# Weight conversion in an attention and two-FFN kernel: other ticks, engines and queues for its steps

## The chip, the cores and the metric
The kernel runs on one core of a Trainium2 chip. The metric is the device time of one execution in microseconds (us). PE is the matrix engine, DVE, ACT and POOL are the vector, scalar and GpSimd engines, and SP is the engine that issues nearly all DMAs; DMA engines move the data on their own.

## The reference
Three stages follow each other. Attention over 4 batches of 8 heads: 32 global and 512 local positions with 64 numbers each; a global query sees everything, a local query sees the global keys and a window of 32 positions to each side. Then a feed-forward net with the square of a ReLU, and another whose activation is a rational function:

```python
    out_g = np.matmul(sm(s_g), v_all)
    mask = np.abs(pos[:, None] - pos[None, :]) <= window
    s_ll = np.where(mask, s_ll, -1000000000.0)
    a_l = sm(np.concatenate([s_lg, s_ll], axis=-1))
    out_l = np.matmul(a_l, np.concatenate([v_g, v_l], axis=2))
...
    x = np.ascontiguousarray(attn_out.transpose(0, 2, 1, 3)).reshape(B * S, H * D)
    r = np.maximum(x @ w_in, 0.0); x = (r * r) @ w_out
    P = a[0] + a[1] * h + a[2] * h2 + a[3] * h3
    Q = 1.0 + np.abs(b[0]) * np.abs(h) + np.abs(b[1]) * h2
    g = P / (Q + 1e-06); return g @ w_out
```

There are 2176 tokens, the model width is 512 and the inner width 2048. The weights arrive as 64-bit floats.

## The kernel before, in words
**Stages.** Attention runs in 40 groups i (0 to 39), five for each of eight half batches n of four heads: four groups of 128 local positions and one for the global queries. For each group do_S makes scores, ACT exponentials (L705, L729, L730), do_T transposes, do_PV multiplies by v, and do_xT transposes the result into xT, the tokens of the FFNs. prep transposes q and k of a later half batch; ACT copies the results (L661, L664, L666). From i = F0 = 11 on a "fill job" of FFN1 is mixed into each group (f_h, f_low, f_y), for the first 5 of 16 chunks f of the inner width; each fifth one, at i = 16, 21, 26 and so on, copies its sums to two tiles pk (L502, one by DVE, one by ACT) and stores them to a DRAM buffer, park (L503). FFN1 (76 jobs) and FFN2 (96 jobs) are then run by step(k), one job a step: do_h multiplies a chunk of w_in with 384 tokens, relu2 or rat_a, rat_b, rat_c compute the activation on ACT and DVE, do_y multiplies with w_out.

**Weights.** PE works with a weight as two parts, hi and lo. A chunk f has two halves, and each half is an item that goes through a pipeline. A "wide" item is loaded with its 64-bit words (L131, tile S), and ACT takes the upper words' absolute value (L138, tile T), POOL scales the lower words (L146), DVE clamps, shifts and puts the sign back (L141, L152, L156), POOL adds (L161), ACT makes hi (L170) and the engine cv["lo"] makes lo (L176): POOL during attention, DVE afterwards. Items that are needed only later are "spilled": the f32 result is stored to DRAM (L166) and loaded again as an "f32" item (L127), for which only hi and lo are left to do. NSET says up to which chunk of FFN1 this is done in attention.

**What sets the order.** cv_tick advances the pipeline. Every cv["per"] ticks a new item is loaded (w_load), and each item runs a step when its age in ticks is the number in its table: OX at first, OE from group 15 on, OL for wide items in the FFNs, OS for f32 items. A group of attention has 4 ticks up to i = 14, then 2 or 3; a step of the FFNs has as many as step says in `ticks`. All T tiles, and the two pk tiles too, come from one pool, cv3, of four slots, so a step that needs a slot waits for the last user of it. Each engine runs its instructions in the order in which they are written. DMAs share eight completion semaphores; one that reuses a semaphore waits for the landing of the DMA that used it last.

**First loads.** The string "kGqAgKQB" orders them: k of half batch 0, k of the global positions, q, v in nine parts (L550, L551, L553), q of the global positions, k and q of half batch 1, then four copies of v within SBUF (L559 to L562), all issued by SP.

Of the kernel before, what the change touches and what calls it, by code (L numbers as in the profile page):

```python
# [9 lines left out]
F32 = mybir.dt.float32  # L10
# [3 lines left out]
ALU = mybir.AluOpType  # L14
# [9 lines left out]
def kernel(  # L24
# [17 lines left out]
    B, H, SL, D = q_l.shape  # L42
    SG = q_g.shape[2]
    T = SL + SG
# [3 lines left out]
    NF = DFF // 128  # L48
# [3 lines left out]


    NPRE, NPART, NSUB = 5, 1536, 256
    NSET = 11
    REST = (384, 256)
    GRP = (384, [384] * 5 + [256])
    NMAX = 384
# [1 line left out]
    pe, ve, sc, gp, sy = nc.tensor, nc.vector, nc.scalar, nc.gpsimd, nc.sync  # L60
# [111 lines left out]
    def w_lo(it):  # L172
        ph, f, half = it["k"]
        if not it["spill"]:
            w = wt[ph, f]
            cv["lo"].tensor_tensor(out=w[:, 1, half], in0=it["T"], in1=w[:, 0, half].bitcast(F32), op=ALU.subtract)  # L176
            done.add(it["k"])

    pools["a"] = wpre
    done = set()  # L180
    todo, line, cv = [], [], dict(z=0, n=0, at=None, per=4, lo=gp)

    def items(ph, fs, mode, spill=False):
        return [dict(k=(ph, f, half), mode=mode, spill=spill) for f in fs for half in range(2)]
# [4 lines left out]
    if wide:  # L189
        back, new = items(0, range(NPRE, NSET), "f32"), items(0, range(NSET, NF), "wide")  # L190
        mixed = back[:6] + new[:1] + back[6:8] + new[1:2] + back[8:] + new[2:]
    else:
        mixed = items(0, rest, "f32")
    plan = [items(0, some, "wide" if wide else "f32"), items(0, range(NPRE, NSET), "wide", True) if wide else [],
            mixed, items(1, rest, "wide", True) if wide else [],
# [3 lines left out]
    LEFT = [sum(len(x) for x in plan[i + 1:]) for i in range(6)]  # L199
# [2 lines left out]

    OX = dict(abs=8, elow=8, clamp=9, shift=9, sign=9, add=10, hi=16, lo=18)
    OE = dict(abs=4, elow=4, clamp=5, shift=6, sign=6, add=8, hi=11, lo=13)
    OL = dict(abs=2, low=3, clamp=3, shift=4, sign=4, add=5, hi=7, lo=9)
    OS = dict(hi=5, lo=8)
# [19 lines left out]
    def cv_idle():  # L228
        return not (todo or line)
# [156 lines left out]
    N1 = sum(j[0] == 0 for j in jobs)  # L386
# [3 lines left out]
    def step(k):  # L390
        last, late = False, []

        if k < NR + 3:
            ticks, stage = (6 - (k > 5) if len(todo) > LEFT[2] else 2), (2 if k < NF else 3)
        elif k < N1 - (NF - NPRE) + 3:
            ticks, stage = 2, 4
        else:
            ticks, stage = (0 if cv_idle() else 6), 5
        left = LEFT[stage]
        if k < NJ:  # L400
            ph, gi, t0, n, f, _, last, _ = jobs[k]
            while (ph, f, 1) not in done:
                cv_tick(left)
            do_h(k)
        if k == N1:
            wide_s.close()
            pools["t"] = ctx.enter_context(tc.tile_pool(name="tmp", bufs=2, side="right"))
        if k + 1 < NJ and last:
            for z in range(1, NK):
                x_split(*jobs[k + 1][:4], z)  # L410
        elif k + 4 < NJ and jobs[k + 4][5]:
            x_split(*jobs[k + 4][:4], 0)


        lag = [2 if y < N1 else 3 for y in ys[:2]]
        if ys and ys[0] <= k - lag[0]:
            do_y(ys.pop(0))
            lag.pop(0)
        while ys and (ys[0] <= k - lag[0] or (last and lag[0] == 2 and ys[0] < k)):
            do_y(ys.pop(0))  # L420
            lag.pop(0)
            lag.append(2 if ys and ys[0] < N1 else 3)
        if k < NJ:
            if ph == 0:
                late = list(relu2(k, k < NF))
                ys.append(k)
            else:
                rat_a(k)
        if N1 <= k - 1 < NJ:
            rat_b(k - 1)  # L430
        if N1 <= k - 2 < NJ:
            rat_c(k - 2)
            ys.append(k - 2)
        while outs:
            outs.pop(0)()

        for t in range(ticks):
            if late and t == 1:
                late.pop(0)()
            cv_tick(left)  # L440
        for f in late:
            f()
# [63 lines left out]
    with ExitStack() as at:  # L506
# [11 lines left out]
        raw1 = wpre.tile([128, 2, 2, 512], F32R, tag="w3", name="raw1").bitcast(F32)  # L518
        raw1 = raw1[:, 0].rearrange("p a (c h d) -> p (a c) h d", h=4, d=D)

        def load_qk(n, i):

            b, hq = divmod(n, 2)
            src, dst, nm = ((q_l, qraw, "qr"), (k_l, kraw, "kr"))[i]
            t = raw1 if n == 1 and not i else raw.tile([128, 4, 4, D], F32, tag=nm, name=nm, bufs=1 + i)
            x = src[b, 4 * hq:4 * hq + 4].rearrange("h (p c) d -> c p h d", c=4)
            for c in range(4):
                sy.dma_start(t[:, c], x[c])
            dst[n] = t


# [8 lines left out]
        def load_v(n, part):  # L540
            b, hq = divmod(n, 2)
            hs = slice(4 * hq, 4 * hq + 4)
            w = vw[n % 2]
            wf = w.rearrange("p w h d -> p w (h d)")
            A, Bw, C = wf[:, 0:5], wf[:, 5:10], wf[:, 10:14]
            vg = v_g[b, hs].rearrange("h g d -> g h d")
            vl = v_l[b, hs]
            if part == 0:
                for a in range(5):
                    sy.dma_start(w[0:96, a, :, 0:D], vl[:, 96 * a:96 * a + 96].rearrange("h p d -> p h d"))  # L550
                sy.dma_start(w[96:128, 9, :, 0:D], vl[:, 480:512].rearrange("h p d -> p h d"))  # L551
                for p, a in ((96, 0), (64, 5), (32, 10)):
                    sy.dma_start(w[p:p + 32, a, :, 0:D], vg)  # L553
                return
            if part == 2:
                for p, t, m in ((96, A, 4), (64, Bw, 4), (32, C, 3)):
                    gp.tensor_copy(t[p:p + 32, 1:], t[p:p + 32, 0:1].to_broadcast([32, m, 4 * (D + 1)]))
                return
            sy.dma_start(Bw[0:64], A[32:96])  # L559
            sy.dma_start(Bw[96:128, 0:4], A[0:32, 1:5])  # L560
            sy.dma_start(C[0:32], A[64:96, 0:4])
            sy.dma_start(C[64:128], A[0:64, 1:5])  # L562
# [13 lines left out]
        for i, pair in enumerate(some):  # L576
            for h in range(4):
# [15 lines left out]
        gr = [wpre.tile([128, 2, 2, 512], F32R, tag="w4", name="gr0").bitcast(F32).rearrange("p a b c -> p (a b c)"),  # L593
              fill(0)]
        gr = [t[0:SG, 0:H * B * D] for t in gr]

        def load_g(i):
            sy.dma_start(gr[i].rearrange("g (x d) -> g x d", d=D), (q_g, k_g)[i].rearrange("b h g d -> g (b h) d"))

        for c in "kGqAgKQB":  # L600
            if c in "qk":
                load_qk(0, "qk".index(c))
            elif c in "QK":
                load_qk(1, "QK".index(c))
            elif c in "gG":
                load_g("gG".index(c))
            else:
                load_v(0, "ABR".index(c))

        ve.memset(xT[:, 0, 0:512], 0.0)  # L610
        wu = bank("PV")
# [58 lines left out]
        F0 = 11  # L670
# [151 lines left out]
        pend = {}  # L822
        cv["at"] = OX

# [11 lines left out]
        for i in range(NS + 1):  # L836
# [55 lines left out]
                sc.activation(coef[:, 6:8], coef[:, 4:6], AF.Abs)  # L892
            if i == F0 + NPRE - 1:
                cv["at"] = OE
            for _ in range(4 if i < F0 + NPRE - 1 else 2 + i % 2):
                cv_tick(LEFT[1])
        do_xT(NS - 1)
        f_y(len(fjobs) - 1)
# [6 lines left out]
    fs.close()  # L905
    cv.update(at=OL, per=3)
    pools["b"] = ctx.enter_context(tc.tile_pool(name="wrest", bufs=1))
    cv["lo"] = ve
    turns.update(y=[2, 5, 3, 6, 4, 7])
    for k in range(NJ + 3):  # L910
        step(k)
# [31 lines left out]
```

## Time and profile before
| | us |
|---|---|
| median of 3 runs | 944.23 (943.25 to 944.95) |
| profiled execution | 944.41 |
| its span | 942.6 |
| PE busy | 900.1 (95%) |
| DVE busy | 722.5 (77%) |
| ACT busy | 611.9 (65%) |
| POOL busy | 156.9 (17%) |

The span is cut into windows, and in each the busy time of the engines is compared with the length of the window; where PE stands still, the timeline says in brackets for how long and which instruction released it. Attention ends at about 242 us, FFN1 at about 540 us.

### The profile page before, as it was taken

Reading aid. Unit: us, or ns where it says so; the run is one execution under the profiler, and the core shown is the slowest. Engines: PE = TensorE matmul, PEld = TensorE weight load, DVE = VectorE, ACT = ScalarE, POOL = GpSimd, SP = SyncE. Lnnn points to the kernel's source line nnn. Section 1 sums busy time; section 2 is a strip of 40 time slices with the busy share of each in tenths; the row PEclk is TensorE's granted clock in tenths of the full one; section 3 lists DMA queues with packets and bytes.
Section 4 is the critical chain, followed back from the end, with each engine's and each line's share of the span. In section 5 each row is a group of like instructions: output and inputs, shape, how many; then the busy total and the mean of one; then the engine's idle time right before and its main releaser. Section 6 shows DMA issues by size and latency. Waiting matters only on the chain.

```text
span 942.6 us, 19526 instructions
## 1 busy us (share of the span) xinstructions
PE 900.1 (95%) x7440; PEld 817.6 (87%) x7440; DVE 722.5 (77%) x1668; ACT 611.9 (65%) x1312; POOL 156.9 (17%) x183
## 2 busy tenths in 40 slices
PE   7869899999999999999999979999999999999997
PEld 4647797989998999999999969888889889888875
DVE  3697876765479576566765598998999999999996
ACT  3567566654677564545554587877777877777875
POOL 5286533310023132221220000000000000000000
PEclk9888999999999999999999999999999999999999
DMA  9999879520555256252421410010010010010010
GB/s 191 194 205 192 201 175 245 149 66 24 158 135 154 88 163 204 90 199 70 148 87 56 133 46 1 1 34 1 1 34 1 1 34 1 1 34 1 3 32 23
DMA packets 101741, 84.21 MB, mean 89 GB/s; under 512 B 60176, under 2 KB 87312, under 8 KB 101648
## 3 DMA queue, kind: packets, MB, share of 16 engines
q1 hardware_dynamic: 101648, 82.97, 33.6%
q8 instruction: 58, 0.95, 0.5%
q14 instruction: 35, 0.29, 0.1%
HBM read 59.51 MB, written 16.52 MB: 81 GB/s over the span
## 4 chain that ended last, share of the span: by engine, by line
PE 70%; DVE 13%; DMA 6%; ACT 5%; issue 2%; SPq 2%; POOL 1%; DVEq 0%; ACTq 0%; POOLq 0%
PE S L286 28%; PE y L364 14%; PE y L361 12%; PE H L471 4%; PE Y L496 4%; DMA S<-in_moe_w_in_dram 2%; PE S L691 2%; DVE big L343 2%; PE PV L785 1%; DVE ts L335 1%; PE tr L658 1%; DVE tq L334 1%; DMA big<-big 1%; DVE T L141 1%; DVE T L156 1%
## 5 line engine op out<-in xcount | busy, mean ns | idle before, releaser
L286 PE MATMUL S<-big,w 128*128 128x384 f32 (+1 forms) x2064 | 364.8, 326 | 1.6 <-ACT big L268 1.1
L286 PEld LDWEIGHTS S<-big,w 128*128 128x128 f32 x2064 | 343.6, 188 | 10.8 <-ACT big L268 1.3
L364 PE MATMUL y<-w,big 128*128 128x512 f32 x816 | 211.0, 398 | 10.2 <-DVE big L343 6.4
L364 PEld LDWEIGHTS y<-w,big 128*128 128x128 f32 x816 | 149.0, 188 | 46.4 <-DVE big L343 16.9
L361 PE MATMUL y<-big,w 128*128 128x384 f32 (+1 forms) x912 | 159.4, 324 | 1.7 <-DVE big L310 1.2
L361 PEld LDWEIGHTS y<-big,w 128*128 128x128 f32 x912 | 149.0, 188 | 2.6 <-DVE big L310 1.9
L161 POOL TENSOR_TENSOR T<-T,S 128x512 uint32<-128x512 uint32 x64 | 88.6, 1384 | 310.0 <-DVE T L156 125.2
L320 ACT ACTIVATE big<-S 128x384 f32<-128x384 f32 (+1 forms) x96 | 45.4, 473 | 83.8 <-PE S L286 73.8
L307 DVE TENSOR_TENSOR big<-big 128x384 f32<-128x384 f32 (+1 forms) x60 | 38.8, 646 | 76.8 <-ACT big L303 76.7
L299 ACT ACTIVATE big<-S 128x384 f32<-128x384 f32 (+1 forms) x76 | 35.4, 466 | 85.1 <-PE S L286 84.5
L323 DVE TENSOR_TENSOR ts<-ts,S 128x384 f32<-128x384 f32 (+1 forms) x96 | 50.8, 529 | 23.5 <-ACT ts L321 23.4
L322 ACT ACTIVATE tq<-big,coef 128x384 f32<-128x384 f32 (+1 forms) x96 | 65.9, 686 | 0.0
L321 ACT ACTIVATE ts<-S,coef 128x384 f32<-128x384 f32 (+1 forms) x96 | 62.3, 648 | 0.0
L324 DVE SCALAR_TENSOR_TENSOR ts<-ts,coef,S 128x384 f32<-128x384 f32 (+1 forms) x96 | 56.8, 592 | 3.4
L303 ACT ACTIVATE big<-big 128x384 fp32r<-128x384 f32 (+1 forms) x76 | 38.2, 503 | 30.3 <-PE y L361 29.7
L138 ACT ACTIVATE T<-S 128x512 f32<-128x512 f32 x64 | 42.8, 670 | 21.8 <-DMA S<-in_moe_w_in_dram 8.9
L336 DVE SCALAR_TENSOR_TENSOR ts<-tq,ts 128x384 f32<-128x384 f32 (+1 forms) x96 | 51.4, 535 | 3.3
L496 PE MATMUL Y<-f,w 128*128 128x256 f32 x360 | 51.4, 293 | 0.0
L310 DVE TENSOR_TENSOR big<-big,big 128x384 fp32r<-128x384 f32 (+1 forms) x76 | 45.8, 603 | 7.2 <-ACT big L305 5.2
L343 DVE TENSOR_TENSOR big<-ts,big 128x384 fp32r<-128x384 f32 (+1 forms) x96 | 50.7, 528 | 0.2 <-ACT big L342 0.2
L325 DVE TENSOR_TENSOR tq<-tq,big 128x384 f32<-128x384 f32 (+1 forms) x96 | 50.7, 528 | 0.0
L471 PE MATMUL H<-f,w 128*128 128x256 f32 x360 | 50.6, 290 | 0.0
(127 smaller groups left out, 1244.9 us busy)
## 6 DMA issues: line engine op xcount, KB each, us to landing
S<-in_moe_w_out_dram SPq DMA_DIRECT2D x32, 512.0 KB, 4.5
scr<-T SPq DMA_DIRECT2D x34, 256.0 KB, 2.2
T<-scr SPq DMA_DIRECT2D x34, 256.0 KB, 2.8
S<-in_moe_w_in_dram SPq DMA_DIRECT2D x32, 256.0 KB, 4.7
S<-in_moe_w_in_dram SPq DMA_DIRECT2D x16, 512.0 KB, 4.0
out_dram<-xT SPq DMA_DIRECT2D x17, 256.0 KB, 2.6
kr<-in_k_l_dram SPq DMA_DIRECT2D x32, 128.0 KB, 5.1
qr<-in_q_l_dram SPq DMA_DIRECT2D x28, 128.0 KB, 4.4
```

The lines of the kernel that those rows point to most:

```text
L161: gp.tensor_tensor(out=u, in0=u, in1=it["S"][:, :, 0], op=ALU.add)
L286: pe.matmul(h, wk[k][s], x[k][t], start=m == 0, stop=m == 3 * NK - 1)
L321: sc.activation(s, h, AF.Identity, scale=coef[:, 3:4], bias=coef[:, 2:3])
L322: sc.activation(q, av, AF.Identity, scale=coef[:, 7:8], bias=coef[:, 6:7])
L323: ve.tensor_tensor(out=s, in0=s, in1=h, op=ALU.mult)
L324: ve.scalar_tensor_tensor(out=s, in0=s, scalar=coef[:, 1:2], in1=h, op0=ALU.add, op1=ALU.mult)
L336: ve.scalar_tensor_tensor(out=s, in0=q, scalar=2.0, in1=s, op0=ALU.subtract, op1=ALU.mult, reverse0=True)
L343: ve.tensor_tensor(out=lo, in0=s, in1=hi.bitcast(F32), op=ALU.subtract)
L361: pe.matmul(y[m][:, 0:n], a, x, start=st and z == 0, stop=sp and z == 2)
L364: pe.matmul(y[m], a, x, start=st and z == 0, stop=sp and z == 2)
L471: pe.matmul(h, w[:, s, 0, 128 * k:128 * k + 128], fx[a, k][t], start=m == 0, stop=m == 3 * NK - 1)
L496: pe.matmul(fy[m // 2][:, NSUB * (m % 2):NSUB * (m % 2) + NSUB], w[:, z % 2, 1, 128 * m:128 * m + 128], (hi, hi, lo)[z], start=f == 0 and ...
```

## The change
Five edits are made at once:
- The first loads are issued from two queues: k, q and v of half batch 0 and the copies stay on SP; k of the global positions, k and q of half batch 1 and q of the global positions are issued by ACT, ahead of everything else that ACT does.
- The counter z starts at 3, so a load is made in the first tick of each group of attention in place of the last, and the table OX counts three ticks more for every step, the first 11 ticks from the load.
- lo (L176) is made by DVE throughout.
- NSET is 12: the two halves of chunk 11 are converted in attention, with one more tick in the even groups after 25, and FFN1 begins with eight wide items and fourteen f32 items in place of ten and twelve. Its steps up to the eighth have 6 ticks.
- At the border to FFN2 three steps have no ticks, and the later ones 3 in place of 6.

```diff
-    NSET = 11
+    NSET = 12
...
-            cv["lo"].tensor_tensor(out=w[:, 1, half], in0=it["T"], in1=w[:, 0, half].bitcast(F32), op=ALU.subtract)
+            ve.tensor_tensor(out=w[:, 1, half], in0=it["T"], in1=w[:, 0, half].bitcast(F32), op=ALU.subtract)
...
-    todo, line, cv = [], [], dict(z=0, n=0, at=None, per=4, lo=gp)
+    todo, line, cv = [], [], dict(z=3, n=0, at=None, per=4)
...
-    OX = dict(abs=8, elow=8, clamp=9, shift=9, sign=9, add=10, hi=16, lo=18)
+    OX = dict(abs=11, elow=11, clamp=12, shift=12, sign=12, add=13, hi=19, lo=21)
...
-            ticks, stage = (6 - (k > 5) if len(todo) > LEFT[2] else 2), (2 if k < NF else 3)
+            ticks, stage = (6 - (k > 8) if len(todo) > LEFT[2] else 2), (2 if k < NF else 3)
...
-            ticks, stage = (0 if cv_idle() else 6), 5
+            ticks, stage = (0 if cv_idle() or N1 <= k < N1 + 3 else 6 if k < N1 else 3), 5
...
-        def load_qk(n, i):
+        def load_qk(n, i, q=sy):
...
-                sy.dma_start(t[:, c], x[c])
+                q.dma_start(t[:, c], x[c])
...
-        for c in "kGqAgKQB":
...
+        load_qk(0, 1)
+        load_g(1, sc)
+        load_qk(0, 0)
+        load_qk(1, 1, sc)
+        load_v(0, 0)
+        load_g(0, sc)
+        load_qk(1, 0, sc)
+        load_v(0, 1)
...
-            for _ in range(4 if i < F0 + NPRE - 1 else 2 + i % 2):
+            for _ in range(4 if i < F0 + NPRE - 1 else 2 + (i % 2 or i > 25)):
```

Four places show how this moves instructions. The first is ACT from its first instruction to its first copy for kt; f and gr are the tiles of the global positions, raw is q of half batch 1.

```order
-L938 UNCONDITIONAL_BRANCH
+L937 UNCONDITIONAL_BRANCH
+L598 DMA f_246<-in_k_g_dram 32x32x64
+L528 DMA kr<-in_k_l_dram 128x4x64 x4
+L598 DMA gr_245<-in_q_g_dram 32x32x64
+L528 DMA raw_109<-in_q_l_dram 128x4x64 x4
 L614 ACT_TABLE_LOAD
 L664 COPY kt_318<-tr 128x5x96
```

Ten DMA issues now stand ahead of the table load and the first copy.

The second is ACT at the park of group 16, before: the park copy, one abs, the exponentials.

```order
L502 COPY pk<-Y 128x512
L138 ACTIVATE T<-S 128x512
L705 ACTIVATE s<-s,nmx 128x128 x4
L664 COPY kt_2066<-tr 128x5x96
L666 COPY kt_2066<-tr 128x32
```

And the same place now.

```order
L502 COPY pk<-Y 128x512
L138 ACTIVATE T<-S 128x512 x2
L705 ACTIVATE s<-s,nmx 128x128 x4
L664 COPY kt_2072<-tr 128x5x96
L666 COPY kt_2072<-tr 128x32
```

A second abs has moved up to the park copy. The third place is ACT at the park of group 21, before, with what each instruction waits for (DMAHW and a number is one of the eight completion semaphores).

```order
L814 COPY xT<-tr 128x4x4x32 [waits PE_49]
L502 COPY pk<-Y 128x512 [waits DMAHW2_49,PE_49,Pool_49]
L138 ACTIVATE T<-S 128x512 [waits DMAHW1_49,DMAHW4_49,DMAHW0_49,DVE_49]
L729 ACTIVATE sg<-S,nmx 128x384
L730 ACTIVATE sg<-S,nmx 128x160
```

And now.

```order
L814 COPY xT<-tr 128x4x4x32 [waits PE_49]
L502 COPY pk<-Y 128x512 [waits DMAHW2_49,DMAHW6_49,DVE_49,PE_49]
L138 ACTIVATE T<-S 128x512 [waits DMAHW4_49,DMAHW7_49,DMAHW3_49,Activation_49]
L729 ACTIVATE sg<-S,nmx 128x384
L730 ACTIVATE sg<-S,nmx 128x160
```

The instructions are the same, but the second pk tile now takes the slot of the first: L502 waits for the store of the first (semaphore 6), and L138 for the store of the second (semaphore 7), where before L138 waited for the first store alone (semaphore 4). The fourth place is DVE at the border to FFN2, from the last sums of FFN1 (L371) to the first low part of the rational function (L343), before.

```order
L371 TENSOR_TENSOR xT<-y,xT 128x384 x4
L176 TENSOR_TENSOR w_7302<-T,w_7302 128x512 x2
L323 TENSOR_TENSOR ts<-ts,S 128x384
L324 SCALAR_TENSOR_TENSOR ts<-ts,coef,S 128x384
L325 TENSOR_TENSOR tq<-tq,big_4384 128x384
L334 SCALAR_TENSOR_TENSOR tq<-tq,tr 128x384
L335 SCALAR_TENSOR_TENSOR ts<-ts,coef,tr 128x384
L336 SCALAR_TENSOR_TENSOR ts<-tq,ts 128x384
L343 TENSOR_TENSOR big_4383<-ts,big_4383 128x384
L176 TENSOR_TENSOR w_7353<-T,w_7353 128x512 x2
```

And now.

```order
L371 TENSOR_TENSOR xT<-y,xT 128x384 x4
L323 TENSOR_TENSOR ts<-ts,S 128x384
L324 SCALAR_TENSOR_TENSOR ts<-ts,coef,S 128x384
L325 TENSOR_TENSOR tq<-tq,big_4405 128x384
L334 SCALAR_TENSOR_TENSOR tq<-tq,tr 128x384
L335 SCALAR_TENSOR_TENSOR ts<-ts,coef,tr 128x384
L336 SCALAR_TENSOR_TENSOR ts<-tq,ts 128x384
L343 TENSOR_TENSOR big_4404<-ts,big_4404 128x384
```

The pairs of L176 are gone from there; later there is one of them in each job.

## Rows read from the trace of the kernel before

**Rows 1.** The page, busy time, share of the span, instructions of each engine.
```profile
PE 900.1 (95%) x7440; PEld 817.6 (87%) x7440; DVE 722.5 (77%) x1668; ACT 611.9 (65%) x1312; POOL 156.9 (17%) x183
```

**Rows 2.** Windows: their length, each engine's busy time, clock, DMA share, GB/s.
```profile
0.00:20.00 20.00, 15.45 (x185) 9.25 (x186) 6.60 (x49) 7.97 (x21) 12.37 (x54) 1.00 1.05 185
...
80.00:100.00 20.00, 19.81 (x332) 17.14 (x331) 18.16 (x51) 14.04 (x38) 14.36 (x16) 1.00 1.04 228
...
160.00:180.00 20.00, 20.00 (x369) 18.16 (x369) 14.24 (x62) 13.48 (x37) 7.76 (x9) 1.00 0.76 186
...
280.00:300.00 20.00, 18.76 (x107) 18.11 (x106) 19.69 (x27) 15.31 (x30) 9.08 (x6) 1.00 0.54 154
540.00:560.00 20.00, 15.46 (x82) 13.78 (x80) 17.57 (x34) 16.01 (x31) 0.00 (x0) 1.00 0.20 69
```

**Rows 3.** Timeline of ACT at the start: start, length, [idle before, releaser].
```profile
0.74 1.28 ACT L614 ACT_TABLE_LOAD   x1 [0.74 <-PEq L927]
9.38 0.56 ACT L664 COPY kt<-tr 128x480 f32<-128x480 f32 x1 [7.36 <-PE tr L658]
```

**Rows 4.** Timeline of SP at the start (a length is that of issuing).
```profile
13.71 2.30 SPq L528 DMA_DIRECT2D raw<-in_q_l_dram  x4
16.13 0.60 SPq L559 DMA_DIRECT2D big<-big  x1
...
18.76 3.01 SPq L528 DMA_DIRECT2D kr<-in_k_l_dram  x4
```

**Rows 5.** DMA issues of 0 to 30 us: KB each, median us to landing.
```profile
big<-big SPq DMA_DIRECT2D x1, 325.0 KB, 5.8
```

**Rows 6.** Timeline of PE in attention, where it had stood still.
```profile
22.71 0.32 PE L785 MATMUL PV<-big,pt 128*32 128x65 f32 x8 [1.98 <-DMA big<-big]
24.44 0.64 PE L785 MATMUL PV<-big,pt 128*32 128x65 f32 x8 [1.40 <-DMA kr<-in_k_l_dram]
...
114.31 0.66 PE L811 MATMUL tr<-ident,xs 128*128 128x128 f32 x4 [2.19 <-ACT kt L666]
...
143.91 1.38 PE L691 MATMUL S<-kt,qt 64*32 64x128 f32 x32 [1.98 <-ACT sg L729]
```

**Rows 7.** Waits of ACT, 20 to 160 us: us in total, times, longest.
```profile
ACT T L138 <- DMA park<-pk: 6.0, 2, 3.2
ACT T L138 <- DMA S<-in_moe_w_in_dram: 4.7, 4, 1.6
...
ACT T L138 <- DMA S<-in_moe_w_out_dram: 3.4, 1, 3.4
```

**Rows 8.** Timeline of ACT behind the park copy of group 21.
```profile
142.72 0.66 ACT L138 ACTIVATE T<-S 128x512 f32<-128x512 f32 x1 [3.17 <-DMA park<-pk]
143.29 0.56 ACT L729 ACTIVATE sg<-S,nmx 128x384 f32<-128x384 f32 x1
...
146.67 0.69 ACT L138 ACTIVATE T<-S 128x512 f32<-128x512 f32 x1 [1.27 <-DMA S<-in_moe_w_in_dram]
```

**Rows 9.** L176 and L141 by line: ns (mean, or min/median/max).
```profile
L176 POOL TENSOR_TENSOR w<-T,w 128x512 fp32r<-128x512 f32 x10 | 13.4, 1335 | 0.0
...
L176 DVE TENSOR_TENSOR w<-T,w x54: 677/684/1806, 247.5 to 560.5; 128x512 fp32r<-128x512 f32 x54
...
L141 DVE TENSOR_SCALAR T<-T x9: 416/891/1346, 51.7 to 96.0; 128x512 f32<-128x512 f32 x9
```

**Rows 10.** Waits of SP's queue, 0 to 80 us.
```profile
SPq L131 <- POOL w L176: 2.5, 3, 1.6
```

**Rows 11.** Timeline of PE at the start of FFN1, where it had stood still.
```profile
293.48 0.97 PE L361 MATMUL y<-big,w 128*128 128x384 f32 x4 [0.97 <-DVE big L310]
298.25 0.96 PE L361 MATMUL y<-big,w 128*128 128x384 f32 x4 [0.27 <-DVE big L310]
304.03 2.18 PE L286 MATMUL S<-big,w 128*128 128x384 f32 x11 [0.48 <-DVE w L176]
```

**Rows 12.** Timeline of DVE at the border to FFN2.
```profile
550.16 1.28 DVE L176 TENSOR_TENSOR w<-T,w 128x512 fp32r<-128x512 f32 x2
```

**Rows 13.** Timeline of PE at that border, where it had stood still.
```profile
550.85 1.67 PE L364 MATMUL y<-w,big 128*128 128x512 f32 x6 [1.56 <-ACT big L342]
555.14 0.97 PE L364 MATMUL y<-w,big 128*128 128x512 f32 x3 [2.62 <-DVE big L343]
```

More of the change, by code (lines that the diff above doesn't have):

```diff
@@ L595, with load_g @@
         gr = [t[0:SG, 0:H * B * D] for t in gr]
-        def load_g(i):
-            sy.dma_start(gr[i].rearrange("g (x d) -> g x d", d=D), (q_g, k_g)[i].rearrange("b h g d -> g (b h) d"))
-        for c in "kGqAgKQB":
[L601 to L608, printed above, removed]
+        def load_g(i, q):
+            q.dma_start(gr[i].rearrange("g (x d) -> g x d", d=D), (q_g, k_g)[i].rearrange("b h g d -> g (b h) d"))
+        load_qk(0, 1)
[6 more added lines that the diff above has]
+        load_v(0, 1)
         ve.memset(xT[:, 0, 0:512], 0.0)
@@ L907 @@
     pools["b"] = ctx.enter_context(tc.tile_pool(name="wrest", bufs=1))
-    cv["lo"] = ve
     turns.update(y=[2, 5, 3, 6, 4, 7])
```

## The prediction
> **What bounds the kernel now.** I read the busy line first: PE works 900.1 of 942.6 us [rows 1]. So only the 42 us in which PE stands still, and the stretches in which the clock is low, can be won, and every new stall of PE is lost in full unless something later waits anyway. Next the table of 20-us windows [rows 2]: at 160 to 180 us PE is busy 20.00 of 20, so a delay that exists at 160 us stays to the end of attention. At 0 to 20 us PE has 15.45, with a DMA share of 1.05 at 185 GB/s: the start waits for transfers. At 80 to 100 us PE (19.81) and DVE (18.16) are both nearly full. At 280 to 300 us (start of FFN1) DVE has 19.69, and at 540 to 560 us (border to FFN2) PE has only 15.46. Then I went to each place and read what released PE, in the timelines of PE, ACT, DVE and SP, and the waits by engine. Five places are touched by the change; I take them in order of time.
>
> **Part 1, first loads on two queues.** Before, SP issued all loads; ACT loaded its function table at 0.74 us (1.28 us) and made its first copy at 9.38 [rows 3]. Now ten DMA issues stand ahead of both on ACT. There are eight completion semaphores for the DMAs, and a DMA that reuses one waits until the last user has landed; such a wait holds ACT, and behind it are the table load and every copy that S(0) needs. The last of the ten waits for the second of the three small v DMAs on SP. From issue to landing I take 5 us: the first raw DMA is issued at 13.71, and kr of the third half batch (issue 18.76) waits for its landing [rows 4]. That v DMA, issued before 11 us, lands about 16, so ACT's first copy comes at about 17.5: 8 us late, and S(0) with it. What hides it: PE stood 1.98 and 1.40 us at the first PV for the copies and kr [rows 6], so 8.1 - 3.4 = 4.7 us are left there. Behind that, L138 (abs) on ACT waits for weights until 70 us: 4.7 us for w_in, of which 1.3 lie later, at 146.67, and 3.4 for w_out [rows 7, 8], 6.8 in all. A late ACT finds those landed, so the 4.7 us are eaten up by 70 us if the transfers keep their time. They don't quite: kr of the third half batch now waits for the landing of the copy L559, which was issued at 16.13 [rows 4] and landed 5.8 later [rows 5]; with half a microsecond gained ahead of it, 15.6 + 5.8 = 21.4 against 18.76, 2.6 late, of which the transfers then in flight hide a part. Bytes are the same and the engines were full, so two queues bring nothing by themselves. I take **+1.5**, from -1.0 (the copies go sooner and PE's 3.4 us go) to +4.7 (nothing absorbs).
>
> **Part 2, 11 ticks.** The load is moved from the last of a group's four ticks to the first; abs, add and the rest stay at the same tick. The order of ACT and POOL is the same up to the fourteenth item, only SP issues a few rows sooner. This alone I cost at nothing: those transfers are bound by bandwidth. What it does is that from i = 15 on every item runs three ticks sooner than before, and that lets its tiles T collide with the two park tiles, which live in the same four slots.
>
> At i = 16 two abs stand in a row behind the park copy. Before one did, and L138 waited for the store in both groups with parks, 6.0 us together, the longer 3.2 [rows 7]; PE stood 2.19 us at 114.31 [rows 6]. Now the second abs (0.66 us by [rows 8]) waits for the second store, about half a microsecond behind the first, as long as one issue (L559's 0.60 in [rows 4]) takes. **+0.8**, from +0.3 (the second has landed) to +1.9 (two copies and an issue).
>
> At i = 21 both park tiles get the same slot. Before, copies went to two slots, and the abs waited 3.17 us for the first store; exp (L729) came behind it at 143.29 and freed the bank for which PE stood 1.98 us [rows 6, 8]. Now ACT's park copy waits for the first store, and the abs behind it for the second: the second wait comes on top, **+3.2**. PE is full afterwards [rows 2], so all of it is on the path. From +2.0 (a store that lands as fast as PE's own stall of 1.98 suggests) to +4.4 (with a copy and an issue of 0.6 each).
>
> **Part 3, low parts on DVE.** Ten L176 go from POOL (1335 ns) to DVE (684 ns) [rows 9], between 50 and 104 us. DVE gets 10 x 0.684 = 6.8 us more in queue. Against that, DVE's other work is stretched beside POOL: L141 takes from 416 to 1346 ns there, 891 in the middle [rows 9]. For its nine that is 9 x 0.475 = 4.3 us; L152 is the same form of work, so I put the stretching at twice that, 8.6 us, and L176 at four tenths of it, 3.4 us, by my estimate, since POOL runs an addition, a scaling and copies beside it. That leaves DVE 3.4 us more to do in 54 us, which I cost at nothing, as it waits in part of them. And three loads waited 2.5 us for L176 to free a tile [rows 10]; these go sooner. Of that I take a third, **-0.8**, from -2.5 (all those waits) to +1.6 (five L176 in 80 to 100 us, 3.4 us, less the 1.8 us that DVE had free there).
>
> The Trainium skill ("SBUF — State Buffer", section "SBUF: two separate sides") says that DVE and GpSimd share a port pair that whoever starts first holds for the whole instruction, the other fully blocked. By that rule each L176 on POOL could cost DVE its full length, and the sum would fall as in the third rival below; the stretch of L141 up to 1346 ns agrees with it, its shortest of 416 shows that many ops meet no lock.
>
> **Part 4, twelve chunks made in attention.** Two more conversions in attention, after i = 25, where PE is full and the others are not (the row of 160 to 180 us: DVE 14.24, ACT 13.48, [rows 2]): **0**, up to +0.6 if an abs meets a store. At the start of FFN1 eight f32 conversions instead of ten; DVE, full there, loses two of them. PE's stalls there are 0.97, 0.27 and 0.48 [rows 11], all behind DVE: **-1.5** of 1.72, from -1.7 to -0.5 (the reloads that replace them use L176 as well).
>
> **Part 5, no reloads at the border.** For three jobs no reload runs, then three ticks a job instead of six. Before, two L176 a job lie on DVE ahead of the rational chain (1.28 us at 550.16, [rows 12]); PE stood 1.56 at 550.85 behind ACT's L342 and 2.62 at 555.14 behind DVE's L343 [rows 13]. ACT comes to L342 about 0.5 sooner, without the hi copies ahead, and L343 1.2 sooner (one pair): **-1.7**. From -2.2 (more of the 4.18 us goes) to -0.8 (the pair only moves behind, where one L176 a job still stands beside PE's step).
>
> **Sum.** +1.5 + 0.8 + 3.2 - 0.8 + 0 - 1.5 - 1.7 = +1.5 us. The profiled execution took 944.41 us (span 942.6), the median of the runs is 944.23, so 945.9 by the one and **945.7** by the other. Something of 0.2% (1.9 us) is the least that a measurement of this kernel can tell from no change: faster is below 942.3, slower above 946.1.
>
> **Rivals.**
> *The start isn't absorbed* (slower). The waits of L138 that are to swallow the delay end when a load lands. If the loads wait in turn for tiles that a late ACT and POOL free, they slip with it, and the 4.7 us stay: 945.7 - 1.5 + 4.7 = 948.9. It decides itself where L138 waits as long as before in spite of the late start. For it: L131 waited for POOL [rows 10], so the coupling is there. Against: 2.5 us only.
> *Attention hides all its moves* (faster), the parks' among them. If the second store lands as fast as the first, or PE's work behind the parks has slack that I don't see, the terms of the start, the parks and L176 come to nothing, and 3.2 us of the two FFN borders are left: 944.2 - 3.2 = 941.0. For it: PE waits for transfers at the start anyway [rows 6]. Against: the 20.00 of 160 to 180 us.
> *The shared port* (faster). If DVE's work between 50 and 104 us is on PE's path and every L176 on POOL blocked it, the move saves 10 x (1335 - 684) ns = 6.5 us in place of 0.8: 945.7 + 0.8 - 6.5 = 940.0. Against: PE has 19.81 of 20 at 80 to 100 us, so DVE hardly held it.
> *The 11 ticks do nothing*: this is in the forecast for the first fourteen items; if it held for i = 16 and 21 as well, the 4.0 us of the parks would go, 941.7. The order of instructions speaks against it.
>
> **How the numbers follow.** Forecast 0.45, start not absorbed 0.22, attention hides all (the parks as before among it) 0.18, shared port 0.08, and 0.07 for what I don't see, half each way. The forecast's own range is 943 to 948.5, and some three tenths of it lie above 946.1, hardly any below 942.3. Slower: 0.22 + 0.45 x 0.3 + 0.03 = 0.38; faster: 0.18 + 0.08 + 0.02 = 0.28; the same: 0.34. The range must reach both neighbours: 940.8 to 950.0.
>
> **What would show it.** After the change: first copy of ACT at 17 to 18 us and S(0) at about 21; L138's waits before 70 us mostly gone; at i = 21 a wait of ACT ahead of L502 for a store and another ahead of L138, with PE standing about 5 us; DVE below 19 of 20 at 280 to 300 us and no stall of PE on DVE there; at the border PE's two stalls below 2.5 us together. I am wrong if the start's delay is still there at 76 us, if the wait ahead of L502 isn't there, or if the stalls at the borders return some jobs later.

## The result, and where the time went

The changed kernel takes 956.54 us (954.98 to 957.1), the kernel before 944.59 (943.25 to 945.13); the ratio is 1.0111, with an interval of 1.0091 to 1.0131. It is slower by about 11 us, outside the range of the prediction. The profiled execution has a span of 954.2 us, 11.6 more than before.

Busy times hardly moved, so the difference is standing and clock. The page's line of the changed kernel (engine, busy us, share of the span), to be read beside [rows 1]:

```profile
PE 902.4 (95%) x7440; PEld 821.8 (86%) x7440; DVE 718.8 (75%) x1678; ACT 611.8 (64%) x1310; POOL 146.9 (15%) x175
```

PE runs the same instructions in the same order in both kernels. So the lag of the changed kernel can be read at each of them: the start of a matmul after the change less its start before. The places are named by their time before the change.

| place | lag, us |
|---|---|
| first S, 12.6 | 11.4 |
| 75.2 | 0.4 |
| 103.3, ahead of the park of group 16 | 2.3 |
| 117.2, behind it | 9.4 |
| 143.9, behind the park of group 21 | 12.9 |
| 245.2, FFN1 has begun | 14.4 |
| 306.7, its conversions are over | 13.2 |
| 591.3, FFN2 is under way | 11.5 |

Three fifths of the final lag come in the 14 us between the third place and the fourth. The timeline of PE in the changed kernel, where it had stood still (start, length, in brackets the idle time and what released it), beside [rows 6], [rows 11] and [rows 13]:

```profile
20.48 1.97 PE L658 MATMUL tr<-ident,qr 128*128 128x128 f32 x8 [10.54 <-ACT kt L666]
...
73.42 0.66 PE L811 MATMUL tr<-ident,xs 128*128 128x128 f32 x4 [2.01 <-ACT qt L661]
...
81.43 0.66 PE L785 MATMUL PV<-big,pt 128*32 128x65 f32 x32 [1.68 <-DVE xs L796]
...
121.58 1.12 PE L811 MATMUL tr<-ident,xs 128*128 128x128 f32 x4 [7.13 <-ACT kt L666]
...
141.76 0.66 PE L811 MATMUL tr<-ident,xs 128*128 128x128 f32 x4 [1.52 <-ACT qt L661]
156.82 1.33 PE L691 MATMUL S<-kt,qt 64*32 64x128 f32 x32 [3.96 <-ACT sg L729]
...
193.26 0.65 PE L811 MATMUL tr<-ident,xs 128*128 128x128 f32 x4 [1.21 <-ACT kt L666]
...
308.05 0.96 PE L361 MATMUL y<-big,w 128*128 128x384 f32 x4 [0.21 <-DVE big L310]
...
564.43 1.66 PE L364 MATMUL y<-w,big 128*128 128x512 f32 x6 [1.21 <-ACT big L342]
567.87 0.95 PE L364 MATMUL y<-w,big 128*128 128x512 f32 x3 [1.77 <-DVE big L343]
```

The stall at 121.58 is the one that stood at 114.31 with 2.19 us in [rows 6]. Followed back, it leads from PE to ACT, from ACT to a park store, and from the store to SP. ACT in the changed kernel, around the park of group 16: the park copy, then two abs that wait 6.94 us for a store, and behind them in ACT's order the copy L664/L666 for which PE waits:

```profile
110.89 0.59 ACT L502 COPY pk<-Y 128x512 f32<-128x512 f32 x1 [0.99 <-POOL S L146]
118.42 1.42 ACT L138 ACTIVATE T<-S 128x512 f32<-128x512 f32 x2 [6.94 <-DMA park<-pk]
119.75 1.26 ACT L705 ACTIVATE s<-s,nmx 128x128 f32<-128x128 f32 x4
120.91 0.54 ACT L664 COPY kt<-tr 128x480 f32<-128x480 f32 x1
121.35 0.18 ACT L666 COPY kt<-tr 128x32 f32<-128x32 f32 x1
```

SP at the same place after the change (a length is that of issuing):

```profile
105.47 0.60 SPq L166 DMA_DIRECT2D scr<-T  x1
109.95 0.35 SPq L131 DMA_DIRECT2D S<-in_moe_w_out_dram  x1
110.40 3.67 SPq L550 DMA_DIRECT2D big<-in_v_l_dram  x5
114.16 0.43 SPq L551 DMA_DIRECT2D big<-in_v_l_dram  x1
114.64 1.37 SPq L553 DMA_DIRECT2D big<-in_v_g_dram  x3
116.11 0.90 SPq L503 DMA_DIRECT2D park<-pk  x2
```

And before the change:

```profile
102.64 0.60 SPq L166 DMA_DIRECT2D scr<-T  x1
103.34 2.75 SPq L550 DMA_DIRECT2D big<-in_v_l_dram  x5
106.18 0.43 SPq L551 DMA_DIRECT2D big<-in_v_l_dram  x1
106.66 2.48 SPq L553 DMA_DIRECT2D big<-in_v_g_dram  x3
109.61 0.90 SPq L503 DMA_DIRECT2D park<-pk  x2
110.60 0.45 SPq L131 DMA_DIRECT2D S<-in_moe_w_out_dram  x1
```

The load L131 has moved from behind the park stores to ahead of the nine v loads. There SP stands at it from 106.07 to 109.95, 3.9 us, and everything queued behind goes out later: the first store at 116.11 in place of 109.61, 6.5 us, of which 2.3 are the lag that was there already. There SP is held by POOL; these are all its waits of that kind, 100 to 125 us, in the changed kernel (us in total, times, longest), and then in the kernel before:

```profile
SPq L131 <- POOL T L161: 10.9, 3, 4.1
```

```profile
SPq L131 <- POOL T L161: 5.8, 2, 4.3
```

A load needs a tile S that POOL's addition (L161) frees. Before, SP waited for that too, but up to 101.2 us, when the park copies were not yet made (they end at 109.1 and 109.6), and up to 115.7, when both stores had gone. Now it closes a circle: the store stands behind a load that waits for an addition; the abs of the next item waits for the store; and the next load (issued at 122.19) waits for the addition of that item. While PE waits, the granted clock falls (the share of its full clock that PE gets; 1.00 is full): it is 0.62 in the window of 118 to 127 us below (length, each engine's busy time, clock, DMA share, GB/s), and the lag grows from 7.3 to 9.4 us while PE works. In the kernel before the clock was 1.00 from 110 to 126 us.

```profile
118.00:127.00 9.00, 5.42 (x78) 4.76 (x86) 5.35 (x20) 6.54 (x17) 3.66 (x4) 0.62 0.56 135
```

### The profile page after: what moved, and what is told of

Read it like the earlier page. It is cut to its first block, busy times and chain, and to the rows that moved or that the text cites. A ratio compares the mean times of both kernels' runs of the same rounds, so it can differ in the third digit from the quotient of the medians.

```text
span 954.2 us, 19539 instructions
## 1 busy us (share of the span) xinstructions
PE 902.4 (95%) x7440; PEld 821.8 (86%) x7440; DVE 718.8 (75%) x1678; ACT 611.8 (64%) x1310; POOL 146.9 (15%) x175
## 4 chain that ended last, share of the span: by engine, by line
PE 71%; DVE 14%; DMA 6%; ACT 5%; issue 2%; SPq 1%; POOL 1%; ACTq 0%; DVEq 0%; POOLq 0%
PE S L286 30%; PE y L364 14%; PE y L361 14%; PE Y L496 3%; PE H L471 3%; DMA S<-in_moe_w_in_dram 2%; DVE big L343 1%; PE S L691 1%; PE PV L785 1%; DMA big<-big 1%; DVE ts L335 1%; DVE tq L334 1%; DVE T L156 1%; PE tr L658 1%; DVE big L269 1%
## 5 line engine op out<-in xcount | busy, mean ns | idle before, releaser
L161 POOL TENSOR_TENSOR T<-T,S 128x512 uint32<-128x512 uint32 x64 | 90.6, 1415 | 324.1 <-DVE T L156 218.5
L138 ACT ACTIVATE T<-S 128x512 f32<-128x512 f32 x64 | 43.0, 672 | 25.0 <-DMA park<-pk 9.3
L176 DVE TENSOR_TENSOR w<-T,w 128x512 fp32r<-128x512 f32 x64 | 46.2, 733 | 6.8 <-ACT w L170 6.8
L343 DVE TENSOR_TENSOR big<-ts,big 128x384 fp32r<-128x384 f32 (+1 forms) x96 | 50.8, 529 | 0.2 <-ACT big L342 0.2
```

Source lines behind the costliest of these rows:

```text
L161: gp.tensor_tensor(out=u, in0=u, in1=it["S"][:, :, 0], op=ALU.add)
L343: ve.tensor_tensor(out=lo, in0=s, in1=hi.bitcast(F32), op=ALU.subtract)
```

## The experiments

I held three theories against each other. **Queue**: the load on SP, ahead of the stores, is what is lost. **Slots**: park tiles and T tiles in the same four slots make ACT wait for stores. **Start**: the ten DMA issues ahead of ACT's first copy. The kernels whose names begin with a are the changed kernel with an edit, those with b the kernel before. All ratios are against runs of the kernel before on the same chip. The lags come from each profile and are read at four of the places above; the end of attention, 245 us, is the one to compare. Each lag sets one execution against one: up to 171 us b_border_nset runs the same instructions in the same order as the kernel before on every engine, and has 0.8 us of lag there.

| kernel | median us | ratio and interval | lag at 75 | 103 | 117 | 245 us |
|---|---|---|---|---|---|---|
| changed | 956.54 | 1.0111 (1.0091 to 1.0131) | 0.4 | 2.3 | 9.4 | 14.4 |
| a_ticks8 | 947.06 | 1.0014 (0.9989 to 1.0039) | 1.0 | 2.9 | 4.5 | 3.8 |
| a_park_act | 955.44 | 1.0104 (1.0073 to 1.0135) | 0.4 | 0.7 | 9.1 | 11.1 |
| a_oneq | 954.42 | 1.0104 (1.0076 to 1.0132) | 0.3 | -1.0 | 5.7 | 12.8 |
| a_pk_big | 947.37 | 1.0019 (0.9996 to 1.0041) | 1.1 | 3.0 | 6.8 | 5.2 |
| b_ticks11 | 956.47 | 1.0118 (1.0087 to 1.0149) | 0.0 | -0.1 | 6.2 | 10.1 |
| b_ticks_late | 955.86 | 1.0089 (1.0060 to 1.0118) | 2.1 | 2.0 | 8.1 | 13.3 |
| b_ticks_early | 945.55 | 0.9988 (0.9969 to 1.0006) | -0.7 | -0.1 | -0.2 | -0.3 |
| b_twoq | 951.30 | 1.0043 (1.0028 to 1.0058) | 3.9 | 6.9 | 7.9 | 8.1 |
| b_twoq_lo | 950.36 | 1.0023 (1.0004 to 1.0043) | 1.5 | 3.4 | 5.1 | 4.2 |
| b_lo | 946.17 | 0.9997 (0.9979 to 1.0014) | -1.3 | -3.0 | -0.8 | -1.6 |
| b_border_nset | 943.42 | 0.9980 (0.9962 to 0.9999) | 0.8 | 0.7 | 0.7 | 0.9 |
| b_best | 939.21 | 0.9932 (0.9907 to 0.9956) | -1.5 | -0.8 | -3.2 | -4.8 |
| b_best_lo | 937.49 | 0.9899 (0.9879 to 0.9919) | 1.6 | -0.3 | -2.8 | -4.8 |

**The second part undone (a_ticks8), and alone (b_ticks11).**

```diff
-    todo, line, cv = [], [], dict(z=3, n=0, at=None, per=4)
+    todo, line, cv = [], [], dict(z=0, n=0, at=None, per=4)
-    OX = dict(abs=11, elow=11, clamp=12, shift=12, sign=12, add=13, hi=19, lo=21)
+    OX = dict(abs=8, elow=8, clamp=9, shift=9, sign=9, add=10, hi=16, lo=18)
```

> The changed kernel with the second part alone undone: the counter starts at 0 again and the table has 8, 9, 10, 16, 18. Queue theory (the load that is made three ticks sooner stands on SP ahead of the v loads and the park stores, waits there for a tile that POOL's addition frees, and so delays the stores for which ACT's abs waits, with PE behind it): the stalls of PE at groups 16, 19 and 21 fall back to the sizes of the kernel before, the store at group 16 is issued within 3 us of the park copy, and of the 12 us two thirds to all go: 944 to 948 us. Start theory (ten DMA issues ahead of ACT's first copy, and the low clock behind them, are what is lost): no change, 955 to 957. DVE theory (L176 on DVE holds PE between 75 and 105 us): little change, 953 to 956.

> The kernel before with the second part alone: the counter starts at 3, the table has 11, 12, 13, 19, 21. Queue theory: PE stalls by 6 to 8 us at group 16 as in the changed kernel and the time rises by 8 to 13 us to 953 to 958. Start theory and DVE theory: 943 to 946, no change.

Undone, it leaves a ratio of 1.0014, whose interval includes 1; alone, it gives 1.0118, as much as the whole change. So the second part holds the loss; the start and DVE's part, which a_ticks8 keeps, don't account for it. With the second part undone, PE's stall at group 16 is 2.55 us, near the 2.19 of before:

```profile
117.59 1.11 PE L811 MATMUL tr<-ident,xs 128*128 128x128 f32 x4 [2.55 <-ACT kt L666]
```

**Which half of the second part (b_ticks_early, b_ticks_late).** In the first, the 11 ticks hold for the first fourteen items and the counter returns to 0 at group 15. In the second, only the counter is set to 3 at group 15.

```diff
-                cv["at"] = OE
+                cv.update(at=OE, z=3)
```

> The other half of the second part: 11 ticks for the first fourteen items, and the counter back to 0 at group 15. The order of SP, ACT and POOL is that of the kernel before: no change, 943 to 947. If the loss comes from the first fourteen items: 950 to 957.

> The kernel before with one number set: from group 15 on the counter stands at 3, so that every later load comes three ticks sooner; the first fourteen items run as before. If the loss of the second part comes from the loads that pass the v loads and the park stores there: PE's stalls at groups 16, 19 and 21 as in the changed kernel, and 953 to 957 us (the kernel before, on this chip, near 944 to 946). If it comes from the first fourteen items, loaded sooner against the start's transfers: 943 to 947.

The early half changes nothing that can be measured (0.9988, the interval includes 1), and the late half gives 1.0089. "11 ticks from the load", the part by which the edit is named, is idle. The profile shows how idle: in b_ticks_early every engine runs the same instructions in the same order as in the kernel before, and not even SP's rows have changed places. The side effect on the later items costs the whole, as far as the intervals can tell. PE in the late half alone:

```profile
120.51 1.12 PE L811 MATMUL tr<-ident,xs 128*128 128x128 f32 x4 [6.40 <-ACT kt L666]
140.18 0.66 PE L811 MATMUL tr<-ident,xs 128*128 128x128 f32 x4 [1.21 <-ACT qt L661]
156.10 1.38 PE L691 MATMUL S<-kt,qt 64*32 64x128 f32 x32 [4.81 <-ACT sg L729]
```

**The store on another queue (a_park_act).**

```diff
-                sy.dma_start(park[:, 2 * i:2 * i + 2,
+                sc.dma_start(park[:, 2 * i:2 * i + 2,
```

> The changed kernel, with the park stores issued by ACT in place of SP, so that they don't stand behind the load and the v loads; the slots of the park tiles come out otherwise too. Queue theory: the store at group 16 is issued within 1 us of the copy, ACT's wait of 6.9 us there goes down to 3 or less, and PE's stall of 7.1 to 2 or 3; at group 21 PE's 3.96 falls by 1 to 3; 946 to 951 us in all. Start theory: no change, 955 to 957. Slot theory (the abs has to wait for a store, whatever its queue, and a landing takes some 3 us): 953 to 956.

955.44 us: the slot theory's range, and no gain that can be measured. The timeline of ACT (ACTq: an issue of ACT's queue) shows why:

```profile
110.15 0.39 ACTq L503 DMA_DIRECT2D park<-pk  x1
115.60 0.59 ACT L502 COPY pk<-Y 128x512 f32<-128x512 f32 x1 [7.32 <-DMA park<-pk]
116.22 0.37 ACTq L503 DMA_DIRECT2D park<-pk  x1
```

The first store goes out at once, but in this kernel both park tiles get the same slot already at group 16, so the second copy waits for the first store, and that lands only after 5.5 us (115.60 less 110.15), beside the 512 KB load and the v loads that SP issued in the same microseconds. PE stood 8.47 us there. At group 21, where the tiles got slots of their own, its stall went from 3.96 to 0.34 us. The gain there doesn't reach the time: the lag is 8.2 us at 242 us, against 14.4 in the changed kernel, but PE waits 2.63 us ahead of the first matmul of FFN1 (1.13 in the changed kernel), since ACT now issues the last park's stores ahead of the cast (L268) that this matmul needs, and FFN1 then runs at the slower of the two paces of the last section, 3.3 us from 375 to 540 us. So the queue theory alone falls: the store's place on SP sets how long the wait is, and the shared slots are what makes anyone wait.

**Park tiles elsewhere (a_pk_big).** They go to unused columns of two other tiles, and no abs and no park copy waits for a park store in its profile.

```diff
-            t = cv3.tile([128, 512], U32, tag="T", name="pk").bitcast(F32)
+            t = bigs[i][:, 512:1024]
```

> The changed kernel with the two park tiles in unused columns of two other tiles (big1 and big2, columns 512 to 1023), so that no abs and no park copy waits for a store any more. Slot theory (the waits for the stores are the loss): at group 16 PE's stall of 7.1 us goes to below 2, at group 21 that of 4.0 to below 1, and the time falls by 8 to 11 us to 945 to 948. Queue theory (the load itself, held on SP until POOL frees its tile, comes too late as well): the second abs at group 16 still waits, now for its own load, and PE stalls there by 3 to 5 us; 948 to 952.

947.37 us, ratio 1.0019 in place of 1.0111: nine of the eleven microseconds are gone, though SP's order is that of the changed kernel. What is left of the queue theory shows too. The second abs at group 16 now waits for its own load, the one on which SP stood, and PE stands 3.84 us in place of 7.13:

```profile
116.57 0.66 ACT L138 ACTIVATE T<-S 128x512 f32<-128x512 f32 x1 [3.85 <-DMA S<-in_moe_w_out_dram]
...
118.97 1.12 PE L813 MATMUL tr<-ident,xs 128*128 128x128 f32 x4 [3.84 <-ACT kt L668]
```

(This kernel has two lines more, so L813 and L668 are L811 and L666.) Both halves of the loss are thus shown: the store behind the load, through the shared slots, and the load itself.

**The first part undone (a_oneq), alone (b_twoq), and with the third (b_twoq_lo).** In a_oneq all first loads are issued by SP again, in the order of the kernel before; b_twoq has the first part alone, and b_twoq_lo L176 on DVE beside it.

```diff
-        load_g(1, sc)
+        load_g(1, sy)
...
-        load_qk(1, 1, sc)
+        load_qk(1, 1)
```

> The changed kernel with the first part alone undone: all first loads on SP again, in the order of the kernel before. Queue theory: ACT's first copy is at 9.4 us again, and PE runs 10 us ahead of the changed kernel until 30 us, but at 75 us the lead is below 1 us, since both wait for the same weights there; in the end -1 to +1 us: 955.5 to 957.5. Start theory: the 10 us stay, 945 to 947.

> The kernel before with the first part alone. By the prediction's term +1.5, from -1.0 to +4.7. From the changed kernel, where the 11 us of the start shrink to 0.4 at 75 us and 3 us then come at 80 us with the low clock: +0.5 to +2.5 against the kernel before. If nothing were absorbed: +8 to +12.

> The kernel before with the first and third part. If L176 on POOL is what keeps the late start from being absorbed: ACT's abs waits for L176 no more, the lag against the kernel before is below 2 us at 75 us, as in the changed kernel, and the time is 0 to +2.5 us from that of the kernel before, ratio 1.000 to 1.0025. If it is not: the lag at 75 us stays near 5 us and the ratio near 1.0043.

Undone in the changed kernel it leaves 954.42, a ratio whose interval overlaps that of the changed kernel; by the profiles 1.6 us less lag at 245 us. Alone it costs 0.43%, some 4 us and more than I expected of it: the lag at 75 us is 3.9 us. ACT's abs waits there for L176 on POOL (0.9 us in two waits before), as the waits of ACT, 20 to 90 us, of b_twoq show:

```profile
ACT T L138 <- POOL w L176: 4.2, 6, 0.8
```

With L176 on DVE this line is gone, the lag at 75 us is 1.5 and the ratio 1.0023. So by the profiles the third part pays for about half of what the first costs, and that helps the changed kernel to catch up; the two ratios' intervals overlap. The rest of the difference between b_twoq_lo (4.2 at 245 us) and the kernel before stays a cost of the first part.

**The third part alone (b_lo), the fourth and fifth (b_border_nset).** Their edits are those of the change.

> The kernel before with the third part alone (L176 on DVE in attention). By the prediction's term -0.8, from -2.5 to +1.6: 941.7 to 946. Lock theory (POOL's L176 held DVE up): 938 to 941. If DVE's longer queue holds PE between 50 and 104 us: 946 to 948.

> The kernel before with the fourth and fifth part alone (twelve chunks made in attention, no reloads for three jobs at the border and three ticks a job then). By the prediction's terms: -1.5 - 1.7 and 0 to +0.6 for the extra chunk, 940.5 to 942.5. If the two stretches have stalls that only move behind: 943.5 to 945.

b_lo: no difference in the time that can be measured, and 1.6 us less lag at 245 us in its profile. That speaks against the shared port as a price on PE's path: 6.5 us were to go if each L176 on POOL had blocked DVE and DVE had been on that path. The Trainium skill ("SBUF — State Buffer", section "SBUF: two separate sides") has the port pair locked for the whole instruction, for those operations of DVE that use it. No run here tells whether DVE was blocked, only that PE didn't pay for it. b_border_nset gains 0.2%, at the edge of what can be measured and less than the 3 us that I expected: in its profile the lag of 0.9 us at 245 us is there from 66 us on, ahead of anything that its edit moves; 1.6 are won at the start of FFN1 (0.9 to -0.7), 0.4 come back by 540 us, and 0.9 are won at the border (-0.3 to -1.1), where the changed kernel won 2.4. PE's two stalls are the same in both (1.21 and 1.77 us), but in this profile the clock fell behind them, and the lag rose by 1.5 us there before it fell again (windows as above):

```profile
552.00:556.00 4.00, 2.34 (x9) 2.20 (x10) 3.93 (x9) 3.33 (x7) 0.00 (x0) 0.82 0.02 4
556.00:560.00 4.00, 4.00 (x17) 3.63 (x17) 2.37 (x6) 1.68 (x4) 0.00 (x0) 0.76 0.19 65
```

**What loses nothing, together (b_best, b_best_lo).** The fourth and fifth part with the park tiles in the other tiles, on one queue and with the old ticks; the second has L176 on DVE as well.

> The kernel before with the fourth and fifth part and the park tiles in big1 and big2. Slot theory: PE's stalls of 2.2 and 2.0 us at the parks of groups 16 and 21, and the low clock behind the second, go on top of what the fourth and fifth part give: 937 to 939. If an abs meets another wait there: 940 to 942.

> The fourth and fifth part, the park tiles in big1 and big2, and L176 on DVE, with one queue and 8 ticks: the version without the two parts that lose. From the version with L176 on POOL (939.2 us, ratio 0.993) another 1 to 2 us, as the third part alone gained some 2 us of attention: 937 to 938.5, ratio 0.990 to 0.992. If the parks' slack and L176's are the same: no change from 939.2.

b_best takes 939.21 us, at the upper end of what I expected. b_best_lo takes 937.49 us, a ratio of 0.9899 (0.9879 to 0.9919), and beats both kernels. Its PE doesn't stand at all at the park of group 16, where it stood 2.19 before the change, nor where it stood 1.98 at group 21. One group behind the first it stands 0.83 us, behind an abs that waits 2.44 us for a store to scr (the park of group 16, and the next group):

```profile
111.60 0.60 PE L813 MATMUL tr<-ident,xs 128*128 128x128 f32 x4
...
118.59 0.66 PE L813 MATMUL tr<-ident,xs 128*128 128x128 f32 x4 [0.83 <-ACT kt L668]
```

## Why the prediction was wrong, point by point

**The failed step** is in the second part: "The order of ACT and POOL is the same up to the fourteenth item, only SP issues a few rows sooner. This alone I cost at nothing: those transfers are bound by bandwidth." For the fourteen items nothing at all moves, not even on SP (b_ticks_early). But I did not ask the same of SP from group 15 on, though the load there is moved past nine v loads and two park stores, and I did not ask what that load waits for. It waits for POOL's addition, and a queue that issues in order waits with it. Where I put nothing, the runs show this: the store goes out 4.2 us later, ACT waits 6.94 us for it in place of 2.81, and the lag grows by 7.1 us at group 16. In b_ticks_late, where only the order from group 15 on is changed, the ratio is 1.0089. The row for it stood in the trace of before: SP waited 5.8 us for POOL in 100 to 125 us, at places where no store that was ready stood behind it.

**Group 16**, +0.8 in the sum: +7.1 (2.3 to 9.4). The two abs in a row were foreseen, and the wait for the second store, but that wait is all but nothing: the first abs stands for the first store, which is 4.2 us late by SP's order, and the second abs follows it at once (the two take 1.42 us together). The low clock behind the long stall, some 2 us, was not in the sum.

**Group 21**, +3.2: PE's stall rose from 1.98 to 3.96 us, +2.0, the lower bound. ACT waited twice as foreseen, for the first store ahead of the copy and for the second ahead of the abs (timeline of ACT, changed kernel):

```profile
152.72 0.59 ACT L502 COPY pk<-Y 128x512 f32<-128x512 f32 x1 [3.37 <-DMA park<-pk]
155.64 0.66 ACT L138 ACTIVATE T<-S 128x512 f32<-128x512 f32 x1 [2.33 <-DMA park<-pk]
```

The first wait lay where PE still had work: PE stopped at 152.86 only. So what was added is the second, less than the 3.2 that I put for it.

**Other places in attention**, 0 in the sum: the stalls at 141.76 (1.52) and 193.26 (1.21) are new. Behind them stand an abs that waited for a store to scr and one that waited for a load issued behind park stores; the timeline of ACT:

```profile
139.38 0.69 ACT L138 ACTIVATE T<-S 128x512 f32<-128x512 f32 x1 [2.80 <-DMA scr<-T]
...
190.84 0.68 ACT L138 ACTIVATE T<-S 128x512 f32<-128x512 f32 x1 [3.38 <-DMA S<-in_moe_w_in_dram]
```

The first is the second part's once more: b_ticks_late has it, with 1.21 us at 140.18, at group 19, and the fourth part's first extra tick comes at group 26. The second is in no kernel that has the second or the fourth part alone, but in a_oneq (1.24) and a_pk_big (1.06), which have both. So the fourth part's "0" held where it was alone (b_border_nset: no lag added in attention), and the "up to +0.6 if an abs meets a store" was too narrow for the two together.

**The start**, +1.5: in the changed kernel the mechanism held, and its rival fell. ACT loads its table at 18.49 and makes its first copy at 19.78 (I said 17.5), beside [rows 3]:

```profile
16.27 2.18 ACTq L528 DMA_DIRECT2D raw<-in_q_l_dram  x4
18.49 1.28 ACT L614 ACT_TABLE_LOAD   x1 [18.49 <-DMA raw<-in_q_l_dram]
19.78 0.56 ACT L664 COPY kt<-tr 128x480 f32<-128x480 f32 x1
```

S(0) is 11.4 us late in place of 8, and the lag is still 0.4 at 75 us. The waits of L138 for loads did swallow delay: from 20 to 90 us they fall from 6.9 us to 0.6. But 1.8 us of the catching up, from 71 to 75 us, are luck of the clock, which was low there in the kernel before and full in the changed one (windows as above, of before and then of the changed kernel):

```profile
66.00:76.00 10.00, 5.36 (x52) 3.21 (x50) 6.02 (x21) 5.99 (x17) 7.26 (x8) 0.50 1.10 225
```

```profile
66.00:76.00 10.00, 7.63 (x182) 5.26 (x171) 9.86 (x33) 8.06 (x22) 8.41 (x8) 1.00 1.04 222
```

And the first part alone (b_twoq) costs about what the rival gave it, 4.7 us, in part through waits for L176 on POOL in place of those for loads. The Trainium skill ("DMA: Bandwidth & Descriptors", section "Issuing engines are not separate DMA queues") says that starting DMAs from several engines saves only the time of issuing; b_twoq agrees, with 1.0043 and no gain anywhere. Not foreseen were the 3 us that come back from 76 to 78 us (of before), most of them where PE stands 1.68 us behind DVE, and the stretch of low clock behind that (0.91 in the window of 80 to 100 us). With the third part in the sum at -0.8, the two terms gave +0.7 and the lag at 103 us is 2.3; the parts alone show that they must be read together, since POOL's L176 is in the way of catching up (b_twoq, b_twoq_lo).

**Start of FFN1**, -1.5: -1.2 (14.4 to 13.2). The three stalls of [rows 11], 1.72 us, have become one of 0.21, which is the 1.5; the lag fell by less, since the matmuls came at the slower of two paces there (last section; 15.1 at 280 us). From 306.7 to 540 us 0.7 come back (13.2 to 13.9), about half of it by the pace of matmuls of 256 columns (117.8 ns in place of 116.7). **Border**, -1.7: -2.4 (13.9 to 11.5), a little beyond the bound of -2.2. The stalls are 1.21 and 1.77 where they were 1.56 and 2.62 [rows 13], 2.98 together where I said below 2.5, and two of 0.36 and 0.37 behind them, which I had left out, are gone. These steps were right in place and near in size, though in b_border_nset the clock took part of the gain back.

**The sum**, made again with what was measured: 2.3 for the start and the third part, 7.1, 3.5 from 117.2 to 143.9, 1.5 to 245.2, -1.2, 0.7 in FFN1 and -2.4 at the border: 11.5. The chance of "slower" was put at 0.38 (0.39 by its own terms), the largest of the three, but for another reason; the rival that ended there, the start, was not it. That this side came true is luck.

## What to carry to other kernels

When a step is moved in a schedule, write down for every DMA of it what it waits for and what now stands behind it on the issuing queue: a load that waits for a buffer holds back the stores and loads of others, and on an in-order queue that costs more than the bytes do. Pools that are shared between a pipeline and an unrelated writer couple the two; giving two tiles their own place took the ratio from 0.9980 to 0.9932, more than any part of the change gained. An edit of one number may have its effect far from the place that it is named for, so follow the order of every engine to its end.

## What the runs showed of the hardware that I had not expected

The low clock comes with stalls of PE, and at a price: around the 10.54 us at the start the granted clock was 0.52 in 10 to 24 us, and around the 7.13 us at group 16 it was 0.62 in 118 to 127 us (of two levels, 2.4 and 1.2 GHz). The length of a stall alone does not decide it: in the kernel before, the 2.19 us ahead of 114.31 brought no fall, and the 1.98 ahead of 143.91 did (0.57 in 144 to 148 us). The row of the start:

```profile
10.00:24.00 14.00, 3.52 (x12) 2.76 (x12) 0.00 (x0) 3.65 (x7) 4.15 (x7) 0.52 1.03 178
```

In FFN1 the matmuls of 384 columns start either every 173.3 ns or every 176.7, on average of a stretch, in every kernel here and with the same granted clock of 1.00. A stretch keeps its pace, and where the pace changes PE had nearly always just stood still, if only for 0.2 us. The kernel before has 173.3 from 380 to 540 us; a_park_act, b_ticks11, b_lo and b_best have 176.7 there, which costs them 3.3 us or a little more. So many more matmuls run in 100 us of the kernel before:

```profile
400.00:500.00 100.00, 100.00 (x579) 100.00 (x578) 65.75 (x121) 49.21 (x96) 21.82 (x16) 1.00 0.38 124
```

Than in 100 us of a_park_act:

```profile
400.00:500.00 100.00, 100.00 (x568) 100.00 (x567) 63.97 (x117) 49.75 (x97) 22.26 (x16) 1.00 0.36 113
```

The changed kernel has 176.7 from 258 to 308 us, where the kernel before has 173.3 up to 294. That is why the lags of the experiments are read at 245 us and not at the end. What sets the pace, no run here tells.
